# A cosformer attention and SwiGLU kernel: last tokens of a batch pair on alternate partitions, k-z-v head pairs on PSUM banks in turn, four output buffers

## Chip, cores and metric

One core of one Trainium2 chip. The metric is the device time of one execution in microseconds (us), as the median of several. The kernel takes and gives float32; inside it works in bfloat16 with float32 sums.

## The reference

Eight batches of 8 heads, 576 tokens, head size 64, then a SwiGLU layer on the 4608 x 512 result. Cut to what matters:

```python
theta = pi / 2 * pos / S                       # S = 576
q_p = concat(relu(q) * cos(theta), relu(q) * sin(theta))     # 64 -> 128 features
k_p = the same of k
kv  = einsum('bhsf,bhsd->bhfd', k_p, v)        # sum over tokens
z   = k_p.sum(tokens)
x   = (q_p @ kv) / (q_p @ z + 1e-6)            # all heads side by side: 512 columns
xn  = x / rms(x) * rms_g
out = (silu(xn @ w_gate) * (xn @ w_val)) @ w_out             # 512 -> 1536 -> 512
```

576 tokens are four tiles of 128 and a remainder of 64. The remainders of two batches fill one tile of 128.

## The kernel before

Each batch is first "prepared" (k, v and q scaled, the sums `kvz` formed, `nd` = q times kv, x normalised), then goes through the SwiGLU as one block of 512 tokens. The remainders of all batches make a ninth block. The preparation of the next batches is woven into the blocks, so that it hides under the large matmuls (`gval`, `outp`). The parts that matter, with cuts marked `# ...`:

```python
osb_pool = ctx.enter_context(tc.tile_pool(name="osb", bufs=3))      # output buffers
kp = consts.tile([P, NJ + 1, H, F], BF16, name="kp")                # NJ = 4, scaled k
vv = consts.tile([P, NJ + 1, H, DE], BF16, name="vv")               # v and a column of ones

def load_rest(what, src, b, eng):            # 64 tokens of one batch, runs of 256 bytes
    lane = 64 * (b % 2) if what == "q" else 0
    t = rem_pool.tile([P, H, D], FP32, name="rem" + what, tag="rem" + what)
    eng.dma_start(out=t[lane : lane + SR, :, :], in_=src[b, :, SM:S, :].rearrange("h s d -> s h d"))
    raws[what + "r", b] = t

def k_prep(b, c, e_cos=nc.vector, e_sin=nc.vector):      # chunk c == NJ is the remainder
    lanes = slice(0, P) if c < NJ else slice(0, SR)
    # ... two scaled ReLUs into kp[lanes, c]

def kvz(b, h0, n):                           # k-z-v sums, one two-bank PSUM tile
    if h0 == 0:
        kvz_ps[b] = pools["att"].tile([P, 2, 512], FP32, name="kvz", tag="att")
    for h in range(h0, h0 + n):
        for c in range(NJ + 1):
            nc.tensor.matmul(
                kvz_ps[b][:, h // HH, (h % HH) * DE : (h % HH + 1) * DE],   # HH = 4
                lhsT=kp[:, c, h, :], rhs=vv[:, c, h, :], start=(c == 0), stop=(c == NJ))
# kvz_out copies the sums to SBUF (kvzs), partly on ScalarE (A), partly on VectorE (V)

def store(blk, j, acc):
    osb = osb_pool.tile([P, DM], FP32, name="osb", tag="osb")
    nc.scalar.copy(out=osb[:, :], in_=acc[:, :])          # ScalarE
    # ... nc.sync.dma_start(out=..., in_=osb)

# batch 0, at the very start: sums and evictions two heads at a time
for e in range(4):
    kvz(0, 2 * e, 2)
    kvz_out(0, 2 * e, 2, V if e % 2 else A)
# ... block 0 ends with four output tiles finished together:
for j in range(NJ):
    store(0, j, accs[0, j])
```

The engines' instruction orders are as written; waits between engines (semaphores) are put in by the framework.

## Time and profile before

| | before |
|---|---|
| median of the first three runs | 360.37 us (360.0 to 361.02) |
| span of the profiled run | 359.1 us |
| TensorE (PE) busy | 319.7 us, 89% |
| TensorE idle, 0 to 27 us | 17 us |
| TensorE idle, 72 to 117 us | 12 us |

From the page of the kernel before: the table of engines (busy time, share of the span, instructions; PEld loads weights for PE, DVE is VectorE, ACT ScalarE, POOL GpSimd), then the busy tenths of TensorE in 40 equal slices of the span (9 is 90% or more).

```profile
span 359.1 us, 5685 instructions
PE 319.7 (89%) x2096; PEld 160.2 (45%) x2096; DVE 199.0 (55%) x428; ACT 153.4 (43%) x304; POOL 89.2 (25%) x135
...
PE   0459998957877999899999989999999999999994
```

TensorE is the engine to keep busy, and the row of digits shows where it is not: the first three slices, and the 5, 7, 8, 7, 7 from the ninth slice on (72 to 117 us). A gain has to come from there. The same stretch in 9 us steps, kernel before (window; length; then busy us and instructions of PE, PEld, DVE, ACT, POOL; granted clock of TensorE, where 1 is full speed; busy share of the DMA engines; GB/s):

```profile
72.00:81.00 9.00, 4.95 (x17) 1.93 (x17) 2.96 (x6) 5.59 (x10) 0.00 (x0) 0.81 0.86 226
81.00:90.00 9.00, 7.08 (x73) 3.90 (x71) 5.23 (x11) 6.48 (x13) 0.00 (x0) 1.00 0.28 52
90.00:99.00 9.00, 7.39 (x59) 3.55 (x57) 5.58 (x13) 4.11 (x10) 4.30 (x7) 1.00 0.38 128
99.00:108.00 9.00, 7.16 (x39) 3.14 (x38) 7.77 (x17) 5.48 (x11) 3.86 (x6) 1.00 0.77 209
108.00:117.00 9.00, 6.56 (x47) 3.12 (x45) 8.14 (x20) 3.71 (x8) 3.52 (x5) 1.00 0.74 129
```

The timeline of the kernel before names the two large waits in it (start, us, engine, line, operation, tiles, shapes, count; in brackets the idle time before it and what ended it):

```profile
68.11 1.56 ACT L343 COPY osb<-acc 128x512 f32<-128x512 f32 x3 [0.49 <-PE acc L604]
68.73 7.63 SPq L346 DMA_DIRECT2D out_dram<-osb  x4
75.41 0.59 ACT L343 COPY osb<-acc 128x512 f32<-128x512 f32 x1 [5.73 <-DMA out_dram<-osb]
75.89 1.33 ACT L129 ACTIVATE qp<-raw,sin_tab 128x512 bf16<-128x512 f32 x2
76.05 1.86 PE L324 MATMUL vps<-xnT,wv 128*128 128x512 bf16 x4 [4.55 <-ACT osb L343]
...
114.28 0.28 PE L207 MATMUL kvz<-vv,kp 128*128 128x65 bf16 x4
115.12 0.49 DVE L131 TENSOR_SCALAR qpr<-remq,cos_tab 64x512 bf16<-64x512 f32 x1
115.52 0.59 DVE L131 TENSOR_SCALAR qpr<-remq,sin_tab 64x512 bf16<-64x512 f32 x1
116.14 0.48 DVE L131 TENSOR_SCALAR kp<-remk,cos_tab 64x512 bf16<-64x512 f32 x1
116.55 0.47 DVE L131 TENSOR_SCALAR kp<-remk,sin_tab 64x512 bf16<-64x512 f32 x1
117.08 1.26 PE L207 MATMUL kvz<-vv,kp 128*128 128x65 bf16 x36 [2.52 <-DVE kp L131]
```

First: three output copies go through, the fourth finds no free buffer and waits 5.73 us for the first store. ScalarE's later work stands behind it: its next operation starts at 75.89, 7.78 us after the first copy. Second: batch 3's sums do four matmuls (the four full tiles of the first head) and then stand for 2.52 us until VectorE has scaled the remainders. Third, the start of the kernel before: each pair of heads waits for the eviction of the pair before it.

```profile
15.23 0.71 PE L207 MATMUL kvz<-vv,kp 128*128 128x65 bf16 x10 [3.05 <-DVE vv L140]
17.22 0.71 PE L207 MATMUL kvz<-vv,kp 128*128 128x65 bf16 x10 [1.28 <-ACT kvzs L138]
18.38 0.71 PE L207 MATMUL kvz<-vv,kp 128*128 128x65 bf16 x10 [0.45 <-DVE kvzs L140]
19.44 0.71 PE L207 MATMUL kvz<-vv,kp 128*128 128x65 bf16 x10 [0.35 <-ACT kvzs L138]
20.60 0.60 PE L238 MATMUL nd<-kvzs,qpT 128*128 128x65 bf16 x8 [0.45 <-DVE kvzs L140]
```

The third pair (18.38) is the first one in the second bank. Still it waits for VectorE's copy of the second pair, which reads the first bank.

### The profile page before, as it was taken

Reading aid. Unit: us, or ns where it says so; the run is one execution under the profiler, and the core shown is the slowest. Engines: PE = TensorE matmul, PEld = TensorE weight load, DVE = VectorE, ACT = ScalarE, POOL = GpSimd, SP = SyncE. Lnnn points to the kernel's source line nnn. Section 1 sums busy time; section 2 is a strip of 40 time slices with the busy share of each in tenths; the row PEclk is TensorE's granted clock in tenths of the full one; section 3 lists DMA queues with packets and bytes.
Section 4 is the critical chain, followed back from the end, with each engine's and each line's share of the span. In section 5 each row is a group of like instructions: output and inputs, shape, how many; then the busy total and the mean of one; then the engine's idle time right before and its main releaser. Section 6 shows DMA issues by size and latency. Waiting matters only on the chain.

```text
span 359.1 us, 5685 instructions
## 1 busy us (share of the span) xinstructions
PE 319.7 (89%) x2096; PEld 160.2 (45%) x2096; DVE 199.0 (55%) x428; ACT 153.4 (43%) x304; POOL 89.2 (25%) x135
## 2 busy tenths in 40 slices
PE   0459998957877999899999989999999999999994
PEld 0438454424333544444454435544554444444441
DVE  3654686435689587668756956687474222232300
ACT  3625593457464242644534433436343233323221
POOL 0338421400443158026504640540010000000000
PEclk9999999989999999999999999999999999999999
DMA  7899999883377869948995999898022000110023
GB/s 238 179 202 234 300 232 280 247 229 58 116 214 129 138 172 200 192 138 192 229 192 151 181 168 173 195 232 208 31 73 61 29 29 31 46 42 32 30 58 89
DMA packets 64476, 53.59 MB, mean 149 GB/s; under 512 B 45952, under 2 KB 53632, under 8 KB 64448
## 3 DMA queue, kind: packets, MB, share of 16 engines
q0 software_dynamic: 12144, 29.63, 36.0%
q1 hardware_dynamic: 52304, 23.60, 31.3%
q8 instruction: 16, 0.26, 0.3%
q14 instruction: 12, 0.10, 0.1%
HBM read 38.01 MB, written 9.44 MB: 132 GB/s over the span
## 4 chain that ended last, share of the span: by engine, by line
PE 68%; DVE 10%; DMA 8%; ACT 7%; issue 3%; SPq 2%; POOL 1%; ACTq 0%; DVEq 0%
PE gps L324 20%; PE vps L324 20%; PE acc L361 19%; DMA raw<-in_v_dram 6%; PE kvz L207 3%; PE nd L238 3%; DVE hT L333 2%; ACT sil L332 2%; SPq L92 2%; DMA out_dram<-osb 2%; PE acc L604 2%; ACT scr L264 2%; ACT vv L138 1%; DVE kp L131 1%; DVE rec L253 1%
## 5 line engine op out<-in xcount | busy, mean ns | idle before, releaser
L333 DVE TENSOR_TENSOR hT<-vps,sil 128x512 bf16<-128x512 f32 x108 | 74.4, 689 | 115.2 <-PE vps L324 68.0
L324 PE MATMUL vps<-xnT,wv 128*128 128x512 bf16 (+1 forms) x408 | 101.3, 372 | 4.5 <-ACT osb L343 4.5
L324 PE MATMUL gps<-xnT,wg 128*128 128x512 bf16 (+1 forms) x408 | 101.0, 371 | 3.4 <-ACT sil L332 3.4
L361 PE MATMUL acc<-wo,hT 128*128 128x512 bf16 x384 | 96.6, 379 | 0.0
L332 ACT ACTIVATE sil<-gps 128x512 bf16<-128x512 f32 x108 | 63.7, 591 | 59.1 <-PE gps L324 56.5
L324 PEld LDWEIGHTS <-wv 128*128 128x128 bf16 x456 | 44.5, 100 | 55.1 <-issue 5.6
L324 PEld LDWEIGHTS <-wg 128*128 128x128 bf16 x456 | 42.0, 100 | 45.6 <-issue 5.9
L269 POOL TENSOR_TENSOR rs<-ssq,mhalf 128x1 f32<-128x1 f32 x36 | 20.5, 570 | 158.4 <-ACT scr L264 158.4
L361 PEld LDWEIGHTS <-hT 128*128 128x128 bf16 x384 | 37.6, 98 | 45.3
L343 ACT COPY osb<-acc 128x512 f32<-128x512 f32 x36 | 20.8, 584 | 35.0 <-PE acc L361 28.8
L138 ACT CAST vv<-raw 128x512 bf16<-128x512 f32 x28 | 16.0, 618 | 17.4 <-DMA raw<-in_v_dram 17.4
L207 PE MATMUL kvz<-vv,kp 128*128 128x65 bf16 x320 | 13.3, 199 | 9.3 <-DVE vv L140 3.0
L238 PE MATMUL nd<-kvzs,qpT 128*128 128x65 bf16 x256 | 14.3, 200 | 5.9 <-DVE xt_96 L256 2.0
L238 PEld LDWEIGHTS <-qpT 128*128 128x128 bf16 x256 | 12.4, 102 | 14.8 <-issue 3.6
L131 DVE TENSOR_SCALAR qp<-raw,cos_tab 128x512 bf16<-128x512 f32 x32 | 16.2, 518 | 4.0 <-DMA raw<-in_q_dram 4.0
L207 PEld LDWEIGHTS <-kp 128*128 128x128 bf16 x320 | 12.2, 101 | 11.9 <-ACT kp L129 3.2
L92 POOL DMA_DIRECT2D raw<-in_q_dram x20 | 15.5, 779 | 0.3 <-DVE qpr L131 0.3
L92 POOL DMA_DIRECT2D raw<-in_v_dram x20 | 15.2, 763 | 0.4 <-issue 0.4
L131 DVE TENSOR_SCALAR kp<-raw,cos_tab 128x512 bf16<-128x512 f32 x32 | 15.2, 490 | 0.1
L92 POOL DMA_DIRECT2D raw<-in_k_dram x20 | 15.2, 760 | 0.0
L177 PE MATMUL tps<-ident,qp 128*128 128x128 bf16 x64 | 6.3, 264 | 8.3 <-ACT qp L129 8.2
L604 PE MATMUL acc<-wo,hT 128*128 128x512 bf16 x48 | 12.1, 379 | 0.4 <-DVE hT L333 0.4
(79 smaller groups left out, 248.5 us busy)
## 6 DMA issues: line engine op xcount, KB each, us to landing
out_dram<-osb SPq DMA_DIRECT2D x32, 256.0 KB, 2.8
raw<-in_q_dram POOLq DMA_DIRECT2D x16, 256.0 KB, 10.3
raw<-in_k_dram POOLq DMA_DIRECT2D x16, 256.0 KB, 3.7
raw<-in_v_dram POOLq DMA_DIRECT2D x16, 256.0 KB, 5.4
raw<-in_q_dram POOLq DMA_DIRECT2D x2, 1024.0 KB, 13.8
raw<-in_k_dram POOLq DMA_DIRECT2D x2, 1024.0 KB, 15.6
raw<-in_v_dram POOLq DMA_DIRECT2D x2, 1024.0 KB, 16.9
wg<-in_moe_w_gate_dram POOLq DMA_DIRECT2D x3, 512.0 KB, 9.3
```

Of the source, the lines that this page charges most:

```text
L92: eng.dma_start(out=raws[what, b][:, h0 : h0 + n, :], in_=src[b, h0 : h0 + n, 0:SM, :].rearrange("h (p j) d -> p h (j d)", j=NJ),)
L131: nc.vector.tensor_scalar(out=dst, in0=src, scalar1=tab[lanes, col : col + 1], scalar2=0.0, op0=ALU.mult, op1=ALU.max,)
L138: nc.scalar.copy(out=dst, in_=src)
L207: nc.tensor.matmul(kvz_ps[b][:, h // HH, (h % HH) * DE : (h % HH + 1) * DE], lhsT=kp[:, c, h, :], rhs=vv[:, c, h, :], start=(c == 0), stop ...
L238: nc.tensor.matmul(ps[rows, h // HH, (h % HH) * DE : (h % HH + 1) * DE], lhsT=src[:, h, cols], rhs=kz[:, h, :], start=True, stop=True,)
L269: nc.gpsimd.tensor_tensor(out=rs[:, :], in0=ssq[:, :], in1=mhalf[:, :], op=ALU.pow)
L324: nc.tensor.matmul(ps[:, c0 : c0 + n], lhsT=w[:, dt, nn * P : (nn + 1) * P], rhs=xnTs[blk][:, dt, c0 : c0 + n], start=(dt == 0), stop=(dt ...
L332: nc.scalar.activation(out=sil[:, :], in_=gps[:, :], func=AF.Silu)
L333: nc.vector.tensor_tensor(out=hTs[blk][:, nn, :], in0=vps[:, :], in1=sil[:, :], op=ALU.mult)
L343: nc.scalar.copy(out=osb[:, :], in_=acc[:, :])
L361: nc.tensor.matmul(acc[:, :], lhsT=hTs[blk][:, nn, j * P : (j + 1) * P], rhs=wo[:, nn, :], start=(nn == 0), stop=(nn == NNT - 1),)
L604: nc.tensor.matmul(accs[0, j][:, :], lhsT=hTs[0][:, nn, j * P : (j + 1) * P], rhs=wo[:, nn, :], start=(nn == 0), stop=(nn == NNT - 1),)
```

## The change

Its intent: (1) the remainders of a pair of batches are loaded into one tile, one batch on the even partitions and one on the odd, so that k and q are scaled once per pair; v is masked per batch, so that the sums of one batch see zeros for the other; (2) head pairs take the two PSUM banks in turn, so that one pair can be evicted while the next is summed; (3) a fourth output buffer. The core of the diff, cut:

```diff
-    osb_pool = ctx.enter_context(tc.tile_pool(name="osb", bufs=3))
+    osb_pool = ctx.enter_context(tc.tile_pool(name="osb", bufs=4))
-    vv = consts.tile([P, NJ + 1, H, DE], BF16, name="vv")
+    vv = consts.tile([P, NJ, H, DE], BF16, name="vv")
+    vvr = consts.tile([P, 2, H, DE], BF16, name="vvr")
+    mask = consts.tile([P, 2], FP32, name="mask")
@@ load_rest
-        lane = 64 * (b % 2) if what == "q" else 0
-        t = rem_pool.tile([P, H, D], FP32, name="rem" + what, tag="rem" + what)
+        if (what + "r", b // 2) not in raws:
+            t = rem_pool.tile([P, H, D], FP32, name="rem" + what, tag="rem" + what)
+            raws[what + "r", b // 2] = t
+            if b == 0 and what != "q":
+                nc.vector.memset(t[:, :, :], 0.0)
         eng.dma_start(
-            out=t[lane : lane + SR, :, :], ...
+            out=raws[what + "r", b // 2][b % 2 : P : 2, :, :], ...
@@ v_prep, remainder
-        copy(eng, vv[lanes, c, :, 0:D], src)
+            nc.scalar.activation(out=dst, in_=src, func=AF.Copy, scale=mask[:, par : par + 1])
@@ kvz
+            c0 = (h // HH * 2 + h % 2) * DE
-                    kvz_ps[b][:, h // HH, (h % HH) * DE : (h % HH + 1) * DE],
-                    lhsT=kp[:, c, h, :], rhs=vv[:, c, h, :],
+                    kvz_ps[b][:, h // 2 % 2, c0 : c0 + DE], lhsT=kp[:, c, h, :],
+                    rhs=vv[:, c, h, :] if c < NJ else vvr[:, b % 2, h, :],
@@ nd, remainder rows
-                (slice(0, SR), qprT, slice(0, SR), kvzs[b - 1]),
-                (slice(SR, P), qprT, slice(SR, P), kvzs[b]),
+                (slice(0, SR), qprT, slice(0, P, 2), kvzs[b - 1]),
+                (slice(SR, P), qprT, slice(1, P, 2), kvzs[b]),
@@ plan of the preparation
-            if n == NJ and what in ("x", "xn") and b % 2 == 0:
+            if n == NJ and what != "v" and b % 2 == (what in ("q", "k")):
                 continue
@@ block 2, step 1
                 x_of(1, NJ)
+                qr_prep(2)
```

Left out: the loads of both remainders now go with the even batch, the q scaling of the first pair moves to the place of its odd batch, the table of angles follows the new order of tokens, the masks are made at the start, and `kvz_out` follows the banks.

More of the change, by code (lines that the diff above doesn't have):

```diff
@@ L68 @@
     kp = consts.tile([P, NJ + 1, H, F], BF16, name="kp")
-    vv = consts.tile([P, NJ + 1, H, DE], BF16, name="vv")
+    vv = consts.tile([P, NJ, H, DE], BF16, name="vv")
+    vvr = consts.tile([P, 2, H, DE], BF16, name="vvr")
+    par_i = consts.tile([P, 2], mybir.dt.int32, name="par_i")
+    mask = consts.tile([P, 2], FP32, name="mask")
+    half_f = consts.tile([P, 1], FP32, name="half_f")
     xt_ring = [consts.tile([P, DM + 1], FP32, name=f"xt{i}") for i in range(NXT)]
@@ L97, in load_rest @@
     def load_rest(what, src, b, eng):
-        lane = 64 * (b % 2) if what == "q" else 0
-        t = rem_pool.tile([P, H, D], FP32, name="rem" + what, tag="rem" + what)
+        if (what + "r", b // 2) not in raws:
[3 more added lines that the diff above has]
+                nc.vector.memset(t[:, :, :], 0.0)
         eng.dma_start(
-            out=t[lane : lane + SR, :, :], in_=src[b, :, SM:S, :].rearrange("h s d -> s h d")
+            out=raws[what + "r", b // 2][b % 2 : P : 2, :, :],
+            in_=src[b, :, SM:S, :].rearrange("h s d -> s h d"),
         )
-        raws[what + "r", b] = t
     def load(what, src, b):
         load_piece(what, src, b, 0, H, nc.gpsimd)
-        load_rest(what, src, b, nc.gpsimd)
+        if b % 2 == 0:
+            load_rest(what, src, b, nc.gpsimd)
+            load_rest(what, src, b + 1, nc.gpsimd)
     def main(what, b, j):
@@ L140, in copy @@
             nc.vector.tensor_copy(out=dst, in_=src)
+    ALL = slice(0, P)
     def k_prep(b, c, e_cos=nc.vector, e_sin=nc.vector):
-        lanes = slice(0, P) if c < NJ else slice(0, SR)
-        src = main("k", b, c) if c < NJ else raws["kr", b][0:SR, :, :]
-        relu_scaled(e_cos, kp[lanes, c, :, 0:D], src, cos_tab, c, lanes)
-        relu_scaled(e_sin, kp[lanes, c, :, D:F], src, sin_tab, c, lanes)
+        src = main("k", b, c) if c < NJ else raws["kr", b // 2][:, :, :]
+        relu_scaled(e_cos, kp[:, c, :, 0:D], src, cos_tab, c, ALL)
+        relu_scaled(e_sin, kp[:, c, :, D:F], src, sin_tab, c, ALL)
     def v_prep_heads(b, h0, n, eng):
@@ L152, in v_prep @@
     def v_prep(b, c, eng=nc.scalar):
-        lanes = slice(0, P) if c < NJ else slice(0, SR)
-        src = main("v", b, c) if c < NJ else raws["vr", b][0:SR, :, :]
-        copy(eng, vv[lanes, c, :, 0:D], src)
+        if c < NJ:
+            copy(eng, vv[:, c, :, 0:D], main("v", b, c))
+            return
+        par = b % 2
+        dst, src = vvr[:, par, :, 0:D], raws["vr", b // 2][:, :, :]
+        if eng is nc.scalar:
+            nc.scalar.activation(out=dst, in_=src, func=AF.Copy, scale=mask[:, par : par + 1])
+        else:
+            nc.vector.tensor_scalar(
+                out=dst, in0=src, scalar1=mask[:, par : par + 1], scalar2=None, op0=ALU.mult
+            )
     qps = {}
@@ L187, in qr_prep @@
     def qr_prep(b):
-        lane = 64 * (b % 2)
-        lanes = slice(lane, lane + SR)
-        src = raws["qr", b][lanes, :, :]
-        relu_scaled(nc.vector, qpr[lanes, :, 0:D], src, cos_tab, NJ, lanes)
-        relu_scaled(nc.vector, qpr[lanes, :, D:F], src, sin_tab, NJ, lanes)
-        if b % 2 == 1:
-            nc.sync.dma_start_transpose(
-                out=qprT[:, :, :], in_=qpr[:, :, :].rearrange("p h f -> p (h f)")
-            )
+        src = raws["qr", b // 2][:, :, :]
+        relu_scaled(nc.vector, qpr[:, :, 0:D], src, cos_tab, NJ, ALL)
+        relu_scaled(nc.vector, qpr[:, :, D:F], src, sin_tab, NJ, ALL)
+        nc.sync.dma_start_transpose(
+            out=qprT[:, :, :], in_=qpr[:, :, :].rearrange("p h f -> p (h f)")
+        )
     kvzs = {}
@@ L205, in kvz, with kvz_out @@
         for h in range(h0, h0 + n):
+            c0 = (h // HH * 2 + h % 2) * DE
             for c in range(NJ + 1):
                 nc.tensor.matmul(
-                    kvz_ps[b][:, h // HH, (h % HH) * DE : (h % HH + 1) * DE],
-                    lhsT=kp[:, c, h, :], rhs=vv[:, c, h, :],
+                    kvz_ps[b][:, h // 2 % 2, c0 : c0 + DE], lhsT=kp[:, c, h, :],
+                    rhs=vv[:, c, h, :] if c < NJ else vvr[:, b % 2, h, :],
                     start=(c == 0), stop=(c == NJ),
                 )
-    def kvz_out(b, h0, n, eng):
-        g, hh = divmod(h0, HH)
-        copy(
-            eng, kvzs[b][:, h0 : h0 + n, :],
-            kvz_ps[b][:, g, hh * DE : (hh + n) * DE].rearrange("p (h e) -> p h e", e=DE),
-        )
+    def kvz_out(b, bank, eng, pairs=slice(0, 2)):
+        dst = kvzs[b][:, :, :].rearrange("p (a g i) e -> p g a i e", g=2, i=2)
+        src = kvz_ps[b][:, bank, 0 : HH * DE].rearrange("p (a i e) -> p a i e", a=2, i=2)
+        copy(eng, dst[:, bank, pairs, :, :], src[:, pairs, :, :])
     nds = {}
@@ L373 @@
         load_piece("k", k, 0, HH * e, HH, nc.sync)
-    load_rest("k", k, 0, nc.sync)
-    load_rest("v", v, 0, nc.sync)
+    for what, src in (("k", k), ("v", v)):
+        load_rest(what, src, 0, nc.sync)
     for e in range(4):
@@ L392 @@
     nc.vector.tensor_copy(out=iota_f[:, :], in_=iota_i[:, :])
+    nc.vector.tensor_single_scalar(
+        out=par_i[:, 0:1], in_=iota_i[:, :], scalar=1, op=ALU.bitwise_and
+    )
+    nc.vector.tensor_single_scalar(
+        out=par_i[:, 1:2], in_=iota_i[:, :], scalar=1, op=ALU.logical_shift_right
+    )
+    nc.vector.tensor_copy(out=mask[:, 1:2], in_=par_i[:, 0:1])
+    nc.vector.tensor_copy(out=half_f[:, :], in_=par_i[:, 1:2])
+    nc.vector.tensor_scalar(
+        out=mask[:, 0:1], in0=mask[:, 1:2], scalar1=-1.0, scalar2=1.0, op0=ALU.mult, op1=ALU.add
+    )
     ang = math.pi / 2.0 / float(S)
@@ L398 @@
         )
-    for e in range(2):
-        rows = slice(e * SR, (e + 1) * SR)
-        nc.vector.tensor_scalar(
-            out=th_tab[rows, NJ : NJ + 1], in0=iota_f[rows, :], scalar1=float(SM - e * SR),
-            scalar2=ang, op0=ALU.add, op1=ALU.mult,
-        )
+    nc.vector.tensor_scalar(
+        out=th_tab[:, NJ : NJ + 1], in0=half_f[:, :], scalar1=float(SM), scalar2=ang,
+        op0=ALU.add, op1=ALU.mult,
+    )
     nc.vector.tensor_single_scalar(
@@ L409 @@
     nc.scalar.activation(out=cos_tab[:, :], in_=cth_tab[:, :], func=AF.Sin)
-    nc.vector.memset(kp[SR:P, NJ, :, :], 0.0)
-    nc.vector.memset(vv[SR:P, NJ, :, :], 0.0)
-    for c in range(NJ + 1):
+    for c in range(NJ):
         nc.vector.memset(vv[:, c, :, D:DE], 1.0)
+    for e in range(2):
+        nc.vector.tensor_copy(
+            out=vvr[:, e, :, D:DE], in_=mask[:, e : e + 1].unsqueeze(1).to_broadcast([P, H, 1])
+        )
     for name, bufs in (("gv", 2), ("acc", 2), ("att", 1)):
@@ L438 @@
         kvz(0, 2 * e, 2)
-        kvz_out(0, 2 * e, 2, V if e % 2 else A)
+        kvz_out(0, e % 2, V if e % 2 else A, slice(e // 2, e // 2 + 1))
     def first_steps(j):
@@ L470 @@
     gval_end(0, 1)
-    load_rest("q", q, 0, nc.gpsimd)
     for what, src in (("q", q), ("k", k), ("v", v)):
         load(what, src, 1)
+        if what == "q":
+            load_rest(what, src, 0, nc.gpsimd)
+        load_rest(what, src, 1, nc.gpsimd)
     for s in range(3):
@@ L489, in loads_of @@
         load_piece(what, src, b, n * e, n, nc.gpsimd)
-        if e == cut - 1:
+        if e == cut - 1 and b % 2 == 0:
             load_rest(what, src, b, nc.gpsimd)
+            load_rest(what, src, b + 1, nc.gpsimd)
     def plan_of(**whats):
@@ L520 @@
     PLAN_2 = plans(
-        4, q=((0, (0, 1)), (1, (2, 3)), (3, (4,))), k=((2, (0, 1)), (3, (2, 3)), (4, (4,))),
+        4, q=((0, (0, 1)), (1, (2, 3))), k=((2, (0, 1)), (3, (2, 3)), (4, (4,))),
         v=((2, (0, 1)), (3, (2, 3)), (4, (4,))),
@@ L544, in before @@
             elif what == "kvz_out":
-                kvz_out(b, 0, HH, A)
-                kvz_out(b, HH, HH, V)
+                kvz_out(b, 0, A)
+                kvz_out(b, 1, V)
             elif what == "x":
@@ L570 @@
     for nn in range(2, NNT):
-        if nn == 5:
-            qr_prep(0)
         if 8 <= nn <= 11:
@@ L580 @@
             k_prep(1, 1, V, A)
-            qr_prep(1)
+            qr_prep(0)
         if nn == 11:
@@ L594 @@
         if nn == 2:
-            kvz_out(1, 0, HH, A)
-            kvz_out(1, HH, HH, V)
+            kvz_out(1, 0, A)
+            kvz_out(1, 1, V)
         if 3 <= nn <= 6:
```

## The prediction

> **What bounds the kernel now.** TensorE: busy 319.7 of 359.1 us (table of engines). By 9 us stretches it is nearly full from 27 to 72 us and, but for about 3 us, from 117 us to the end. It loses 17 us before 27 us (first loads) and about 12 us from 72 to 117 us. The chain of waits names the causes there:
>
> - 68.7 to 75.3 us: block 0's fourth output copy (ScalarE, line 343) waits 5.73 us for the first copy's store, as there are three output buffers. TensorE stands 4.55 us, and its next matmuls take 0.42 instead of 0.216 us (granted clock 0.81).
> - 75.4 to 86 us: ScalarE back to back (scaling, SiLU, casts for batch 2), begun only when the fourth copy is done.
> - 114.3 to 117.1 us: batch 3's k-v sums stop for 2.52 us after four matmuls, waiting for VectorE's scaling of its last tokens: q 2 x 0.49, then k 2 x 0.48 us.
>
> **What the change does.**
>
> 1. Fourth output buffer. The fourth copy starts at about 69.6 instead of 75.4, so ScalarE's stretch, and all behind it, moves forward by about 5.8 us. Batch 2's v (issued 48.7, landing 19.4 later, plus about 1.2 for the rests now ahead of it; estimate from about 210 GB/s) should land by 70 us, before ScalarE wants it at about 74.7. I take 5.5.
> 2. Pair tile. Last q and k are scaled once per pair on 128 partitions: 16 operations of 0.47 to 0.72 us disappear, since 128 partitions cost what 64 do (0.48 against 0.47 in the groups by shape). Most lie under a full TensorE: worth nothing. On the path is batch 3: no k work remains and the q work moves one step earlier, into a VectorE idle of 0.73 us. The 2.52 us wait should go: I take 2.3. The masked v costs ScalarE up to 0.1 us more each, hidden. Loads keep their bytes, but come with the even batch; v of batches 4 and 6, waited for until 143.6 and 212 us, may land up to 0.5 us later.
> 3. Banks in turn. At the start each pair of heads waits for the eviction of the pair before: gaps of 0.35 to 0.45 us. [...]But here the third pair, already in the other bank, waits too (0.45 us), and later VectorE's eviction of one bank waits for ScalarE's of the other (9.7 us in seven). The order seems kept tile-wide: I expect 0, at most 1 us.
>
> **Prediction.** 360.4 - 5.5 - 2.3 - 0.2 = 352.4 us, 80% range 350.3 to 355.5. Faster by over 2%: 0.66; within 2%: 0.32; slower: 0.02.
>
> **What would show it.** No output copy waits for a store; no granted clock below 0.9 from 60 to 90 us; TensorE idle from 72 to 117 us down from 12 to 4 or 5 us; no wait for scaled k before batch 3's sums; operations on the last k halved; the gaps between head pairs at the start unchanged.
>
> **What would make it wrong.** ScalarE waiting for batch 2's v or q transposes, which now meet four stores in the busy DMA stretch after 68 us; later landings of v for batches 4 and 6; or a start slowed because the first remainder loads must follow a memset of their tile.

Its third point's figure, 0, rests on the measured waits (0.45 and 9.7 us).

## The result

| | before | changed |
|---|---|---|
| median, runs of the first comparison | 360.19 us (359.87 to 361.02, 4 runs) | 350.99 us (349.61 to 352.02, 4 runs) |
| ratio, 95% interval | 1 | 0.9739 (0.9701 to 0.9776) |
| ratio in a second comparison, six runs | 1 | 0.9713 (0.9676 to 0.9749) |
| span of the profiled run | 359.1 us | 349.2 us |

A ratio is the mean time of one kernel's fast runs over that of the other's of the same rounds, so it is not quite the ratio of the medians beside it. The time lies inside the predicted range, 1.4 us below the point. All outputs are right.

The page of the changed kernel:

```profile
span 349.2 us, 5640 instructions
PE 316.5 (91%) x2060; PEld 159.5 (46%) x2096; DVE 193.3 (55%) x419; ACT 153.9 (44%) x304; POOL 90.2 (26%) x135
...
PE   1559998979699997999999999999999999999993
```

The same stretch of the changed kernel in 9 us steps, columns as above:

```profile
72.00:81.00 9.00, 6.43 (x61) 3.41 (x61) 5.03 (x10) 7.40 (x14) 0.00 (x0) 0.92 0.74 169
81.00:90.00 9.00, 7.88 (x54) 3.67 (x54) 4.49 (x10) 3.01 (x7) 2.25 (x4) 0.89 0.17 58
90.00:99.00 9.00, 6.62 (x45) 3.04 (x44) 6.52 (x15) 4.92 (x11) 4.50 (x7) 1.00 0.50 160
99.00:108.00 9.00, 8.89 (x55) 4.18 (x55) 8.93 (x22) 4.68 (x11) 1.55 (x3) 1.00 0.78 145
108.00:117.00 9.00, 8.95 (x89) 5.01 (x90) 5.92 (x14) 3.60 (x9) 3.94 (x6) 1.00 1.03 213
```

TensorE's idle time from 72 to 117 us fell from 11.9 to 6.2 us (45 less the sum of the first busy column), and the two steps from 99 us on are full. The timeline of the changed kernel at the places shown before:

```profile
66.36 2.05 ACT L359 COPY osb<-acc 128x512 f32<-128x512 f32 x4 [0.49 <-PE acc L632]
68.28 1.36 ACT L139 ACTIVATE qp<-raw,sin_tab 128x512 bf16<-128x512 f32 x2
...
78.59 0.19 PE L225 MATMUL kvz<-vvr,kp 128*128 128x65 bf16 x1 [1.53 <-ACT vvr L170]
80.14 1.49 PE L340 MATMUL gps<-xnT,wg 128*128 128x512 bf16 x3 [0.22 <-issue]
81.42 1.82 PE L340 MATMUL vps<-xnT,wv 128*128 128x512 bf16 x4
...
105.46 0.48 DVE L141 TENSOR_SCALAR qpr<-remq,cos_tab 128x512 bf16<-128x512 f32 x1
105.85 0.48 DVE L141 TENSOR_SCALAR qpr<-remq,sin_tab 128x512 bf16<-128x512 f32 x1
108.39 0.28 PE L225 MATMUL kvz<-vv,kp 128*128 128x65 bf16 x4
108.51 0.19 PE L225 MATMUL kvz<-vvr,kp 128*128 128x65 bf16 x1
```

Four copies run in one go and ScalarE's next work starts at 68.28 instead of 75.89. Batch 3's sums no longer stop (no bracket at 108.51). New is a slow patch: at 80 to 83 us the matmuls of 512 columns come every 0.43 us instead of every 0.216. In this stretch the granted clock is 0.50 (columns: window; length; PE busy; granted clock; DMA share; GB/s):

```profile
80.00:83.00 3.00, 2.86 (x7) 0.50 0.00 0
```

Laid over each other from mark to mark, the two profiles give this sum. The marks are the starts of the named instruction; the last matmul of a group is taken from the single records of the trace.

| from | to | before | changed | difference |
|---|---|---|---|---|
| start | first output copy | 68.11 | 66.36 | -1.75 |
| first output copy | fourth output copy | 7.30 | 1.44 | -5.86 |
| fourth output copy | last matmul of batch 2's sums | 11.80 | 11.87 | +0.07 |
| that | last matmul of batch 3's sums | 30.93 | 29.90 | -1.03 |
| that | end | 240.95 | 239.62 | -1.33 |
| sum | | 359.1 | 349.2 | -9.9 |

The second line is the predicted one. The first, the fourth and the fifth were open: a start that was predicted unchanged, a batch 3 term of 1.0 instead of 2.3 us, and a gain where a small loss was expected. The experiments were made for these, and to see whether the parts add up.

For four of them (before_osb4, after_osb3, before_banks, after_halves) two profiles are on record. One is quoted below; the other is called the second profile. It shows how far one program differs from itself.

### The profile page after: what moved, and what is told of

Read it like the earlier page. It is cut to its first block, busy times and chain, and to the rows that moved or that the text cites. A ratio compares the mean times of both kernels' runs of the same rounds, so it can differ in the third digit from the quotient of the medians.

```text
span 349.2 us, 5640 instructions
## 1 busy us (share of the span) xinstructions
PE 316.5 (91%) x2060; PEld 159.5 (46%) x2096; DVE 193.3 (55%) x419; ACT 153.9 (44%) x304; POOL 90.2 (26%) x135
## 4 chain that ended last, share of the span: by engine, by line
PE 78%; DVE 7%; DMA 5%; ACT 5%; issue 3%; POOL 1%; SPq 0%; ACTq 0%; DVEq 0%; POOLq 0%
PE gps L340 24%; PE vps L340 23%; PE acc L377 22%; PE nd L254 3%; PE kvz L225 3%; DVE xt L272 2%; DMA raw<-in_v_dram 2%; DMA raw<-in_k_dram 2%; PE tps L196 1%; DMA raw<-in_q_dram 1%; ACT sil L348 1%; DVE hT L349 1%; DVE kp L141 1%; ACT scr L280 1%; ACT kp L139 1%
## 5 line engine op out<-in xcount | busy, mean ns | idle before, releaser
L340 PE MATMUL gps<-xnT,wg 128*128 128x512 bf16 (+1 forms) x440 | 111.5, 371 | 3.5 <-ACT sil L348 2.4
L340 PE MATMUL vps<-xnT,wv 128*128 128x512 bf16 (+1 forms) x450 | 112.4, 371 | 0.4
L377 PE MATMUL acc<-wo,hT 128*128 128x512 bf16 x372 | 94.8, 379 | 0.4
L280 ACT ACTIVATE scr<-xt 128x513 bf16<-128x513 f32 x36 | 22.9, 636 | 60.3 <-DVE xt L272 60.3
L293 DVE SCALAR_TENSOR_TENSOR xn<-xt,rs,gb 128x512 bf16<-128x512 f32 x36 | 26.7, 743 | 1.3 <-POOL rs L285 1.3
L272 DVE TENSOR_TENSOR xt<-nd,rec 128x512 f32<-128x512 f32 x36 | 24.9, 692 | 1.2
L225 PE MATMUL kvz<-vv,kp 128*128 128x65 bf16 x256 | 12.5, 199 | 4.7 <-DVE vv L150 3.3
```

Source lines behind the costliest of these rows:

```text
L225: nc.tensor.matmul(kvz_ps[b][:, h // 2 % 2, c0 : c0 + DE], lhsT=kp[:, c, h, :], rhs=vv[:, c, h, :] if c < NJ else vvr[:, b % 2, h, :], sta ...
L272: nc.vector.tensor_tensor(out=xt[:, 0:DM].rearrange("p (g h d) -> p g h d", g=2, d=D), in0=ndv[:, :, :, 0:D], in1=rec[:, :].rearrange("p ( ...
L280: nc.scalar.activation(out=scr[:, :], in_=xt[:, :], func=AF.Square, scale=DM**-0.5, accum_out=ssq[:, :],)
L293: nc.vector.scalar_tensor_tensor(out=t[:, :], in0=xt[:, 0:DM], scalar=rs[:, 0:1], in1=gb[:, :], op0=ALU.mult, op1=ALU.mult,)
L340: nc.tensor.matmul(ps[:, c0 : c0 + n], lhsT=w[:, dt, nn * P : (nn + 1) * P], rhs=xnTs[blk][:, dt, c0 : c0 + n], start=(dt == 0), stop=(dt ...
L377: nc.tensor.matmul(acc[:, :], lhsT=hTs[blk][:, nn, j * P : (j + 1) * P], rhs=wo[:, nn, :], start=(nn == 0), stop=(nn == NNT - 1),)
```

## The experiments

Ten kernels ran. Ratios are against the kernel before on the same chip.

| run | median us | ratio (95%) |
|---|---|---|
| before_osb4 | 354.57 | 0.982 (0.976 to 0.988) |
| after_osb3 | 357.78 | 0.9888 (0.9816 to 0.9961) |
| before_banks | 360.99 | 0.9995 (0.9944 to 1.0047) |
| after_halves | 351.61 | 0.9736 (0.9691 to 0.9781) |
| before_pad96 | 359.35 | 0.997 (0.9921 to 1.002) |
| after_pad416 | 350.85 | 0.9712 (0.9674 to 0.9749) |
| after_rest_again | 353.35 | 0.9809 (0.9748 to 0.9869) |
| after_kvz_split | 348.73 | 0.9655 (0.9608 to 0.9702) |
| after_again | 350.75 | 0.9713 (0.9676 to 0.9749) |
| split_k_on_vector | 348.43 | 0.9665 (0.9623 to 0.9708) |

### Four buffers alone, and all but the four buffers

before_osb4 is the kernel before with

```diff
-    osb_pool = ... name="osb", bufs=3
+    osb_pool = ... name="osb", bufs=4
```

> The kernel before with four output buffers and nothing else. My theory (the fourth copy held ScalarE's whole next stretch): the fourth copy starts about 0.5 us after the third instead of 5.7 us later, everything behind moves forward by about 5.8 us, batch 3's 2.5 us wait for the scaled last k stays and so does the start: 354 to 355.5 us. Rival (the freed stores and transposes collide in the DMA queues and give it back): over 357 us, with waits for q transposes or for batch 2's v between 68 and 90 us.

Measured: 354.57 us, ratio 0.982, so 1.8% of 360 us or about 6.5 us (estimate from the ratio; its interval reaches from 4.3 to 8.6 us). Its timeline:

```profile
67.78 2.05 ACT L343 COPY osb<-acc 128x512 f32<-128x512 f32 x4 [0.49 <-PE acc L604]
69.70 1.36 ACT L129 ACTIVATE qp<-raw,sin_tab 128x512 bf16<-128x512 f32 x2
```

The start is as before (67.78), the four copies run in one go, and the 2.5 us wait before batch 3's remainder stays, as the waits of TensorE list (`kvz` for VectorE's `kp`, longest 2.5 us). No wait for transposes or for batch 2's v appeared. The rival is out.

after_osb3 is the same line turned round in the changed kernel.

> The changed kernel with three output buffers again. If the parts add up, it loses what the fourth buffer gave, less the slow-clock matmuls that now come after the third batch's sums: 355 to 357 us, and the fourth copy again waits 5 to 6 us for the first store. If the gain of the changed kernel came mostly from the pair tile and the start, it stays below 353.5 us.

Measured: ratio 0.9888, against 0.9739 and 0.9713 of the changed kernel, so three buffers cost 1.5 to 1.75%, 5.4 to 6.3 us. The median of 357.8 us lies above the expected range; it includes a run over 1.5% above the fastest run of its kernel, and the three fast runs are 354.8, 356.4 and 359.2 us. The profile was of the slow run, so its lines are not used. The second profile (span 353.4 us) is not slow, and in it the fourth copy again waits for the first store, as expected; TensorE then stands for 4.08 us:

```profile
73.26 0.59 ACT L359 COPY osb<-acc 128x512 f32<-128x512 f32 x1 [5.26 <-DMA out_dram<-osb]
```

With both runs the fourth buffer is worth about 6 us, whether the rest is there or not: the parts add up, as far as intervals of 4 to 5 us can tell.

### Banks in turn alone

before_banks takes only the new column and bank of each head and the matching `kvz_out`:

```diff
+            c0 = (h // HH * 2 + h % 2) * DE
-                    kvz_ps[b][:, h // HH, (h % HH) * DE : (h % HH + 1) * DE],
+                    kvz_ps[b][:, h // 2 % 2, c0 : c0 + DE],
-        kvz_out(0, 2 * e, 2, V if e % 2 else A)
+        kvz_out(0, e % 2, V if e % 2 else A, slice(e // 2, e // 2 + 1))
```

> The kernel before with the k-z-v head pairs on alternating banks and nothing else. My theory (order between the engines is kept for the whole two-bank tile): the three gaps between head pairs at the start stay at 0.35 to 0.45 us, the first q-times-kv matmul starts 4.2 us after the last v landed as before, and the time is within 0.3% of the kernel before. Rival (the banks gave the 1.3 us that the changed kernel gained at the start): the gaps vanish and the time is about 359 us.

Measured: ratio 0.9995, no difference. The waits between head pairs are still there in before_banks, although every pair is now in another bank than the pair before:

```profile
17.33 0.71 PE L208 MATMUL kvz<-vv,kp 128*128 128x65 bf16 x10 [0.70 <-ACT kvzs L138]
18.50 0.71 PE L208 MATMUL kvz<-vv,kp 128*128 128x65 bf16 x10 [0.45 <-DVE kvzs L140]
19.56 0.71 PE L208 MATMUL kvz<-vv,kp 128*128 128x65 bf16 x10 [0.35 <-ACT kvzs L138]
```

The second profile has the same three waits (0.68, 0.45 and 0.35 us). So the start of the changed kernel did not come from the banks.

### What held the pairs: one tile or two

If the order is kept per PSUM tile, two tiles should do what two banks of one tile did not. after_kvz_split gives batch 0 two one-bank tiles from a pool that is free at that time; the heads go to the same banks in turn.

```diff
-            kvz_ps[b] = pools["att"].tile([P, 2, 512], FP32, name="kvz", tag="att")
+            if b == 0:
+                kvz_ps[b] = [pools["acc"].tile([P, 512], FP32, name="kvz", tag="acc")[:, :]
+                             for _ in range(2)]
+            else:
+                t = pools["att"].tile([P, 2, 512], FP32, name="kvz", tag="att")
+                kvz_ps[b] = [t[:, 0, :], t[:, 1, :]]
```

> The changed kernel with batch 0's k-z-v sums in two one-bank tiles instead of one two-bank tile; banks in turn as before. Theory (the order is kept per tile, so alternate banks of one tile could not overlap): the three gaps of 0.35 to 0.45 us between head pairs vanish, the first q-times-kv matmul comes 1.0 to 1.2 us earlier relative to the first k-z-v matmul (3.3 instead of 4.45 us after it), and the time falls by about 1 us, to about 350 us. Rival (the pairs are held by the v casts or by the bank itself): the gaps stay.

Measured: 348.73 us, ratio 0.9655, which is 0.6 to 0.8% below the changed kernel's ratios, with intervals that overlap. The first q-times-kv matmul comes 2.17 us after the first k-z-v matmul (18.19 less 16.02), even less than the expected 3.3; in the changed kernel it is 4.45 us (19.30 less 14.85). In its timeline the matmuls follow each other without a bracket while both engines evict:

```profile
17.09 0.41 PE L232 MATMUL kvz<-vv,kp 128*128 128x65 bf16 x4
17.31 0.24 PE L232 MATMUL kvz<-vvr,kp 128*128 128x65 bf16 x1
17.32 0.29 DVE L150 CAST kvzs<-kvz 128x130 bf16<-128x130 f32 x1 [1.11 <-PE kvz L232]
```

That settles it for this program: with alternate banks in one tile the pairs wait (0.70, 0.45 and 0.35 us in before_banks), with two tiles they do not, so the waits between engines were set for the whole tile. The idea of the second part of the change was sound, but here it needs two tiles. Besides the three gaps, the last pair's eviction also left the path: the first heads' `nd` need only the sums copied long before.

### What moved the landings at the start: which partitions, and where the buffers begin

In the changed kernel the last v of batch 0 landed at 14.36 us, before at 16.36. First theory: it is the partitions, as 64 neighbouring ones would be loaded more slowly than alternate ones. This was the assumption. after_halves puts the second batch of a pair into partitions 64 to 127 and changes nothing else:

```diff
-            out=raws[what + "r", b // 2][b % 2 : P : 2, :, :],
+            out=raws[what + "r", b // 2][SR * (b % 2) : SR * (b % 2 + 1), :, :],
# and in the masks, angles and columns of nd: p >> 6 and p & 63 for p & 1 and p >> 1
```

> The changed kernel with the pair tile shared by halves (partitions 0 to 63 and 64 to 127) instead of alternate partitions; every engine operation keeps its shape. Theory: [...]at the start the two remainder loads take 2.2 us after the k load as in the kernel before, instead of 1.0 us, the last v lands about 1.5 to 2 us later (near 16 us instead of 14.4), and the time is 1.3 to 3 us above the changed kernel. Rival (the start was luck of one run, or came from the order of the first instructions): landings and time like the changed kernel, within 0.5 us.

Measured: the last v landed at 15.02 us, between the two (in the second profile at 14.45 us), and the time did not differ (ratio 0.9736). Most of the theory fell: the landing went back by at most a third of the difference, and the expected 1.3 to 3 us did not appear. What else differs between the kernels before and after? The constants take another number of bytes, and so the load buffers behind them start elsewhere: in the built programs at 416 bytes past a multiple of 512 before, at a multiple of 512 after. That the start address moves a landing was assumed, too. Two runs put the address and the partitions apart, one unused tile each:

```diff
+    pad = consts.tile([P, 24], FP32, name="pad")      # before_pad96: 96 bytes
+    pad = consts.tile([P, 104], FP32, name="pad")     # after_pad416: 416 bytes
```

> The kernel before with 96 unused bytes per partition behind the constants, so that the buffers of the q, k and v loads start at a multiple of 512 bytes, as they happen to in the changed kernel, instead of 416 bytes past one. Theory (the earlier landings of the changed kernel come from where its buffers start in SBUF, not from the alternate partitions): the last v of batch 0 lands near 15 us instead of 16.4, the waits for v near 145 and 213 us shrink, and the time is 1 to 2.5 us below the kernel before. Rival (the partitions did it): the last v still lands at 16.3 to 16.5 us and the time is within 0.5 us of the kernel before.

> The changed kernel with 416 unused bytes per partition behind the constants: the load buffers start 416 bytes past a multiple of 512, as in the kernel before. Theory (start address): the last v of batch 0 lands at 15.3 us or later instead of 14.0 to 14.4, and the time is 1 to 2.5 us above the changed kernel, 352 to 354 us. Rival (alternate partitions alone): lands at 14.0 to 14.5 us, time 350 to 352 us.

Landing of batch 0's last v in us (issue plus time to landing; one value for each profile, without the one profile in the slow state; second profiles behind the semicolon):

| | buffers start 416 bytes past a multiple of 512 | at a multiple of 512 |
|---|---|---|
| remainders to partitions 0 to 63 | 16.36, 16.41, 16.47; 15.46 (before_osb4), 15.24 (before_banks) | 15.15 (before_pad96), 15.02 (after_halves); 14.45 (after_halves) |
| remainders to alternate partitions | 14.81 (after_pad416) | 14.36, 14.46, 14.05, 13.96, 14.09; 13.86 (after_osb3) |

Both changes together are clear: 15.24 to 16.47 us in one corner, 13.86 to 14.46 in the other, with means 1.9 us apart. How it divides is not. By the means the start address is worth 1.1 us in the upper row and 0.7 in the lower, the partitions 1.2 us on the left and 0.7 on the right. But two profiles of one program differ by 0.6 to 1.2 us, and neighbouring corners meet (15.24 and 15.15; 14.45 and 14.46) or hold a single value. So both may count, and it is not shown for either alone. By what mechanism either would act, no run shows.

The time hardly follows, either. before_pad96 gained 0.3% with an interval across 1, after_pad416 lost nothing. The first `nd` starts at 20.60, 20.67 and 20.72 us in the kernels with both old properties (partitions 0 to 63, 416 bytes; second profiles 19.71 and 19.48), and at 19.30, 20.48 and 19.01 in the two profiles of the changed kernel and in after_rest_again (described below; its start is that of the changed kernel), with 19.73 in the second profile of after_osb3. The means are 0.6 us apart, half of what two profiles of one program differ by (1.2 us in before_banks). The last v is often no longer what comes last: the last q piece landed at 6.73, 7.58 and 6.55 us in the same order as 19.30, 20.48 and 19.01, and the scalings of q and k behind it come before the sums. Where it landed alike, at 7.00 us in the second profile of before_osb4 and at 7.03 in that of after_osb3, the first `nd` started alike too, at 19.71 and 19.73, though the v of the latter had landed 1.6 us earlier.

So the -1.75 us in the table of marks is not shown to be an effect of the change. In after_again, the same program as the changed kernel, the first output copy starts at 68.55 us, later than the 68.11 of the kernel before. These profiles also differ in the time from which TensorE's small matmuls (128 columns) come faster: every 0.107 us at first, and every 0.056 us from about 31.0 us on in the kernel before, from 28.4 in the changed one and from 31.6 in after_again.

### The wait of batch 3

after_rest_again lets batch 3 repeat the k scaling and do the q scaling where it was:

```diff
-            if n == NJ and what != "v" and b % 2 == (what in ("q", "k")):
+            if b != 3 and n == NJ and what != "v" and b % 2 == (what in ("q", "k")):
-                qr_prep(2)
```

> The changed kernel in which batch 3 scales the pair's last k a second time and the last q at its old place, as the kernel before did (same values, right result). Theory: the sums of batch 3 again stop after four matmuls and wait about 2 to 2.5 us for VectorE's scaled k; nothing behind absorbs it, so the time is 2 to 2.6 us above the changed kernel, 352.5 to 354 us. Rival (TensorE would have stood there for another reason anyway, so the saved operations are worth little): under 0.7 us more.

Measured: 353.35 us, ratio 0.9809, that is 0.7 to 1.0% or 2.5 to 3.5 us above the changed kernel (from its ratios 0.9739 and 0.9713). The interval is 1.2% wide and overlaps with theirs, and the runs reach from 351.5 to 356.6 us, so the time alone does not settle it. The wait does; it is back in the timeline:

```profile
106.72 0.28 PE L225 MATMUL kvz<-vv,kp 128*128 128x65 bf16 x4
...
108.84 0.47 DVE L141 TENSOR_SCALAR kp<-remk,sin_tab 128x512 bf16<-128x512 f32 x1
109.37 0.20 PE L225 MATMUL kvz<-vvr,kp 128*128 128x65 bf16 x1 [2.36 <-DVE kp L141]
```

This also explains the 1.0 us of the table of marks. From the last matmul of batch 2's sums to that of batch 3's the profiles take 30.93 us (before), 30.79 (after_rest_again), 28.24 (after_halves, second profile), 28.25 (after_again), but 29.90 (after), 29.86 (after_pad416), 29.68 (after_kvz_split). The last three, and none of the others, have a slow patch like that at 80 to 83 us, in which matmuls of 512 columns come every 0.43 us. Without it the term is 2.7 us (30.93 less 28.25); the slow patch took 1.6 us of it back in the profiled run. There it came behind the wait of 1.53 us for `vvr` at 78.59, but after_rest_again has a wait of 1.5 us for `vvr`, too, and no slow patch: what brings it on is not shown.

### The yardstick again, and a further step

after_again is the changed kernel itself, for its spread. split_k_on_vector is after_kvz_split with one more line:

```diff
-                k_prep(b, n, V, sin_eng)
+                k_prep(b, n, V, sin_eng if n < 2 else V)
```

> The changed kernel once more, as the yardstick for the run beside it and for its own spread. 349.5 to 352.5 us; profiles that show the half clock behind batch 2's sums (about 1.3 us) and profiles that do not are both expected.

> The changed kernel with batch 0's sums in two one-bank tiles and, for batch 2, three of the k scalings (sin part of the last two j and of the last tokens) on VectorE instead of ScalarE. Theory (with four buffers ScalarE's stretch before batch 2's sums still sets the pace: 6.2 of 7 us busy, VectorE 3.8): the sums end about 1.5 to 2 us earlier after the first output copy (11.5 us instead of 13.3), and the time is 2 to 4 us below the changed kernel, 346 to 349 us. Rival (what follows is held by something else): as fast as with the two tiles alone, 348 to 350 us.

after_again: 350.75 us, ratio 0.9713, no slow patch in its profile. split_k_on_vector: 348.43 us, ratio 0.9665. That is a little below the changed kernel (0.9713, intervals overlap), but not below the two tiles alone (0.9655). The theory fell: from the first output copy to the last matmul of batch 2's sums it took 13.03 us instead of 13.28. The chain of waits shows VectorE's k scalings in that stretch where ScalarE's were, with VectorE's own multiply between them, which waits for ScalarE's SiLU (SiLU at 73.06 us, the multiply released at 73.59, the next k scalings at 74.19). The waits for v in later blocks, at 134.2 and 170.4 us, were 2.41 and 1.27 us in this profile and gave back part of what it had. Version to keep: after_kvz_split.

## Why the prediction was right

**The bound.** It named the stretch from 72 to 117 us and two waits in it; taking each away alone, or putting it back, moved the time by about what was said. For the fourth buffer this is clear of the noise; for batch 3 it is the wait, and not the time, that shows it.

**How much of the hit is luck.** The two large terms came to 5.86 and 2.7 us where 7.8 was said. A slow patch, which the prediction did not have, took 1.6 us back in the profiled run, and the first and the last line of the table of marks, which it did not have either, gave 3.1 us that other profiles repeat only in part. The mechanism of the two large terms was right; that the sum lies so near to the measured time is partly luck.

**Fourth buffer, 5.5 us.** Right. 5.86 us from mark to mark, 6.5 us alone (0.982), 5.4 to 6.3 us when taken out of the changed kernel, where the wait came back with 5.26 us. The step that could have failed, transposes and stores meeting in the DMA queues, cost nothing: the fourth copy moved forward and the sums of batch 2 followed at the same distance (11.80 and 11.87 us).

**Pair tile, 2.3 us.** Right in kind and about in size: 2.7 us between the marks without the slow patch, 2.36 us of wait when put back. The prediction said that 16 operations disappear; it is 14 (16 to 10 for k, because batches 0 and 1 still each scale theirs, and 16 to 8 for q), and this did not matter, as only batch 3's were on the path. The masked v costs ScalarE 0.74 instead of 0.62 us, about as estimated (in the kernel before, ScalarE's scalings took 0.72 us and its casts 0.62), but it is not quite hidden: the wait for it before batch 2's sums is 1.53 instead of 1.44 us. The reading of strided columns in `nd` costs nothing that the traces show (weight loads of 110 ns in both).

**Banks in turn, 0.** Right, and the reason is shown twice: the gaps stay with alternate banks in one tile, and vanish with two tiles.

**The step that was off: the start.** "a start slowed because the first remainder loads must follow a memset of their tile" was the only thing that the prediction said of the first loads; it had no gain for them. The memsets were done by 2 us, before the load was issued at 3.86. Instead v landed about 1.9 us earlier on average, with new partitions and new start addresses, which no line of the diff mentions. On average 0.6 us of it is seen at the first `nd`, within the spread of one program, so it stays open whether any of it reached the path.

**Later loads, 0.2 us slower.** Not seen. The wait of TensorE behind batch 4's late v is there in all profiles, with and without the change (1.3 to 2.4 us). The 0.97 us behind batch 6's, which make most of the last line of the table of marks, appear in the profile of the kernel before, but not in those of before_osb4, before_banks and before_pad96; before_osb4 has 0.77 us behind batch 5's instead. So that line is not counted as an effect of the change. Whether loading a pair's remainders together makes v land earlier there is left open.

**What would show it.** Three of six signs failed. The operations on the last k fell from 16 to 10, not by half. "No granted clock below 0.9 from 60 to 90 us" failed: the 9 us step reads 0.89, but within it the clock is 0.50 from 80 to 83 us. Before, such a stretch (0.50 from 76 to 78.8 us) lay where ScalarE set the pace (busy 2.80 of these 2.80 us) and hid it: from the fourth copy to the last of batch 2's sums it took 11.80 us, and 11.82 in the second profile of before_osb4, which has no such stretch. Now it lies where TensorE sets the pace (busy 2.86 of the 3.00 us, ScalarE 0.93). TensorE's idle time fell to 6.2, not to 4 or 5 us. The slow patch is not the reason, as its matmuls count as busy (the 2.86 us, at a granted clock of 0.50), and after_again and after_halves have 5.8 and 6.0 us without it; a part is that only 4.05 of the 4.55 us of the first wait lay behind 72 us.

## What to carry to other kernels

Count the output buffers for a burst of outputs at the end of a stage: with three for four copies, the fourth waited 5.73 us for a store here, and ScalarE's later work started at 75.89 us instead of 68.28. Overlap by PSUM banks did not count here, as the waits were set by tile: look in the trace whether a pair in another bank still waits (0.45 us here), and if so try one tile per bank (no wait in after_kvz_split). When a change moves constants about, compare where the DMA targets start and which partitions they use before giving the credit to the logic of the change (with both changed, v landed 1.9 us earlier here), and profile one program twice before explaining a difference of 1 us (two profiles of one program differed by 0.6 to 1.2 us).
